# First chunk of gated linear attention into four experts: loading keys and values as fp32 by GpSimd's queue, with the whole order of the work searched anew

## The chip, the cores and the metric

The kernel runs on one core of one Trainium2 chip. The metric is the time of one execution on the device in microseconds (us), the median of several executions. The engines are named as in the profile: PE is TensorE's matmul and PEld its weight load, DVE is VectorE, ACT is ScalarE, POOL is GpSimd and SP is SyncE, which here only issues DMAs. DMAs issued by SP go into the queue that the profile calls hardware_dynamic, those issued by POOL into the one that it calls software_dynamic.

## What is computed

A recurrent attention with a forget gate, and behind it a mixture of four experts with dense routing. The inputs and the output are fp32, and the kernel feeds its matmuls in bf16.

```python
# q, k, v, f_logit: (4 batches, 8 heads, 768 steps, 48)
f = 1 / (1 + exp(-f_logit))
for t in range(768):
    state = f[:, :, t, :, None] * state + k[t] (outer) v[t]     # 48 x 48 per batch and head
    y[:, :, t] = q[t] @ state
x = y with the heads side by side                              # 3072 x 384
p = probs / (probs.sum(-1) + 1e-9)
out = sum over 4 experts of p[:, e] * (relu(x @ w1[e]) @ w2[e])   # w1 384 x 1024, w2 1024 x 384
```

## The kernel before

**Tiling.** The 768 steps are cut into six chunks of 128. Within a chunk the recurrence is turned into matmuls, batch by batch (b = 0 to 3): running sums of log f (`pe_cs` with the triangular matrix Up or Ub, and for the first chunk also `pe_cq`), their exponentials on ACT (`exps`, `expq`), scaled copies of q and k (`product`, on DVE or POOL), their transposes on PE (`pe_tp`) and a copy out of PSUM into QK, the 128 x 128 score blocks (`pe_at`) which are evicted with a causal mask (`ev_at`, or a plain copy and then `mask_at` on POOL), and the scores times v (`pe_y`). The state between chunks is kept in Sf and its bf16 copy Sb (`pe_kv`, `ev_kv`, `state`). The outputs y are transposed again (`pe_xt`, `dma_xt` or `dma_xs`) and go into the experts: `mm_h`, `relu`, `mm_o` for the first two chunks, and for later ones forms that save multiplications with sums of blocks (`mm_p1`, `mm_hs`, `mm_l1`, `mm_p`).

**The first chunk (c = 0)** is special, since nothing can hide it. Its loads are cut by batch. f and q come in pairs of neighbouring steps (`PAIRED`), in pieces of 384 bytes. k comes by SP in pieces of 192 bytes. v comes by POOL, which casts it to bf16 in the DMA and writes the tile vb that the matmuls read. POOL's v issues 0 and 1 wait for the landings of k1 and k2 (`GATE`).

**What sets the order.** All work is recorded as a list of about 1,550 operations in a planner (`Plan`), each with a cost per engine, dependencies, and the buffers that it takes and frees. A table of numbers, `RANKS`, gives each operation its place (a letter behind a number also fixes its engine). The planner walks the list in that order, chooses buffers, and then emits the instructions in that order, so that every engine's instruction stream is the table's order. An engine runs its stream strictly in sequence: an instruction that waits holds up all behind it. `ORDER` is the order of the first chunk's loads on SP, `SEQ` that of POOL's DMA issues (v0 to v3 and the first weights w0, w1; w2 to w10 follow).

**Weights.** w0 to w3 are halves of w1 of experts 0 and 1, w4 and w5 are the halves of w2 of expert 0, w6 to w10 are whole matrices. All are cast to bf16 in POOL's DMAs, as they always were. The gate's load of the second chunk (f, batches 1 of the first half) waits for w8.

**Fillers.** `FILLER` places extra matmuls of a constant tile into a spare PSUM bank ahead of named operations on PE: six ahead of cs 0.0 (the first running sum) and four ahead of tpk 0.1. Nothing reads what they write.

Of the kernel before, what the change touches and what calls it, by code (L numbers as in the profile page):

```python
# [11 lines left out]
ALU = mybir.AluOpType  # L12
# [64 lines left out]
)  # L77
FILLER = {"cs 0.0": 6, "tpk 0.1": 4}


class Op:
# [10 lines left out]
class Plan:  # L92
# [20 lines left out]
    def run(self):  # L113
# [7 lines left out]
        for o in done:  # L121
            (e, cost), = o.costs.items()
            t = free_at[e]
# [1081 lines left out]
```

## Time and profile before

| what | value |
|---|---|
| time, median of 3 runs | 286.37 us (286.18 to 286.67) |
| the profiled execution's own time | 285.82 us |
| its span, from the first instruction to the last event | 284.1 us |
| PE busy | 276.0 us, 97% of the span |
| DVE, POOL, ACT busy | 208.7, 185.3, 178.2 us |
| DMA packets | 153688, 41.88 MB |

How to read it: the profile has one row for a stretch of equal instructions, with the start, the length, the engine, the line of the kernel, what is written and from what, and in brackets the engine's idle time just before and what ended it. A matmul's recorded length includes its way through the array, so that matmuls in sequence overlap; the distance between the starts of two rows is what the stretch cost. Idle time of an engine that nobody waits for costs nothing.

### The profile page before, as it was taken

What the parts mean: (1) busy time and instruction counts of PE and PEld (TensorE: products, weight loads), DVE (VectorE), ACT (ScalarE), POOL (GpSimd) and SP (SyncE); (2) the same over time, 40 slices, a digit from 0 to 9 for tenths busy, and PEclk for the clock granted to TensorE, in tenths of its full rate; (3) what the DMA queues carried; (4) which work ended last, traced back from release to release, by engine and by line L of the source; (5) the groups of instructions that cost most, each with busy time, mean ns of one, the idle gap of its engine ahead of it and who ended that gap; (6) DMA issues with size and microseconds to landing.
All of it is one profiled execution on the core that took longest, in us unless ns stands there. A gap on an engine that the chain in (4) does not pass through costs nothing.

```text
span 284.1 us, 8015 instructions
## 1 busy us (share of the span) xinstructions
PE 276.0 (97%) x3228; PEld 241.2 (85%) x3228; DVE 208.7 (73%) x437; ACT 178.2 (63%) x350; POOL 185.3 (65%) x197
## 2 busy tenths in 40 slices
PE   6889999999999999999999999999999999999995
PEld 4678565668788999999998999999999899999995
DVE  5695487797779587769887786686765687857683
ACT  5668235647898848686866867769367456556420
POOL 5799353706699878667729955695656545793761
PEclk9999999999999999999999999999999999999999
DMA  6999999999988999999999999996547015201003
GB/s 156 189 195 205 208 195 200 184 216 181 162 150 159 198 164 208 204 168 184 194 175 207 194 179 218 184 166 124 111 82 160 30 31 76 67 0 59 2 2 111
DMA packets 153688, 41.88 MB, mean 147 GB/s; under 512 B 144028, under 2 KB 152860, under 8 KB 153652
## 3 DMA queue, kind: packets, MB, share of 16 engines
q1 hardware_dynamic: 142404, 34.66, 65.1%
q0 software_dynamic: 11248, 6.72, 16.8%
q8 instruction: 25, 0.41, 0.6%
q14 instruction: 11, 0.09, 0.1%
HBM read 31.51 MB, written 4.72 MB: 128 GB/s over the span
## 4 chain that ended last, share of the span: by engine, by line
PE 84%; DMA 9%; POOL 4%; ACT 1%; DVE 1%; issue 0%; ACTq 0%; POOLq 0%
PE ps_m L646 29%; PE ps_m L531 26%; PE ps_m L574 7%; DMA w_sb<-in_moe_w_dram 7%; PE ps_m L514 6%; PE ps_m L499 4%; PE ps_m L654 2%; DMA f<-in_f_logit_dram 2%; PE ps_m L437 2%; POOL w_sb L312 2%; PE ps_m L464 1%; PE ps_m L460 1%; PE ps_m L347 1%; PE ps_m L470 1%; POOL AT L441 1%; PE ps_m L362 1%
## 5 line engine op out<-in xcount | busy, mean ns | idle before, releaser
L531 PE MATMUL ps_m<-x,w_sb 128*128 128x256 bf16 x672 | 84.3, 273 | 0.0
L531 PEld LDWEIGHTS <-w_sb 128*128 128x128 bf16 x672 | 63.6, 98 | 7.1
L595 ACT ACTIVATE h<-ps_m 128x512 bf16<-128x512 f32 x82 | 46.8, 600 | 24.1 <-PE ps_m L531 23.9
L646 PEld LDWEIGHTS <-S 128*128 128x128 bf16 x576 | 48.2, 98 | 0.8
L673 DVE TENSOR_TENSOR o<-ps_m,o 128x192 f32<-128x192 f32 x91 | 31.1, 353 | 19.1 <-PE ps_m L646 17.3
L646 PEld LDWEIGHTS <-h 128*128 128x128 bf16 x432 | 36.2, 98 | 0.8
L610 POOL TENSOR_TENSOR S<-h 128x1024 bf16<-128x1024 bf16 x14 | 29.7, 2124 | 10.3 <-DVE S L610 6.3
L499 PE MATMUL ps_m<-x,w_sb 128*128 128x128 bf16 (+2 forms) x264 | 35.1, 282 | 0.0
L420 ACT ACTIVATE yb<-ps_m,pn 128x384 bf16<-128x384 f32 x55 | 29.4, 586 | 8.5 <-PE ps_m L464 5.6
L397 POOL TENSOR_TENSOR qk<-q,e 128x384 bf16<-128x384 f32 x18 | 21.6, 1201 | 12.5 <-DVE f L549 3.9
L646 PE MATMUL ps_m<-ts_sb,S 128*128 128x192 bf16 x288 | 29.3, 246 | 0.0
L646 PE MATMUL ps_m<-w_sb,h 128*128 128x192 bf16 x288 | 29.2, 246 | 0.0
L646 PE MATMUL ps_m<-w_sb,S 128*128 128x192 bf16 x288 | 28.7, 246 | 0.0
L499 PEld LDWEIGHTS <-w_sb 128*128 128x128 bf16 x264 | 21.6, 98 | 8.1
L593 DVE TENSOR_SCALAR h<-ps_m 128x512 bf16<-128x512 f32 x30 | 20.6, 688 | 9.6 <-PE ps_m L531 8.5
L453 DVE TENSOR_TENSOR AT<-ps_m,mask 128x512 bf16<-128x512 f32 x40 | 25.6, 682 | 2.1 <-PE ps_m L437 2.0
L510 ACT ACTIVATE h<-ps_m 128x512 bf16<-128x512 f32 x33 | 19.1, 595 | 12.2 <-PE ps_m L499 11.8
L380 ACT ACTIVATE e<-ps_m 128x384 f32<-128x384 f32 x40 | 23.6, 708 | 3.2 <-PE ps_m L347 1.4
L610 POOL TENSOR_TENSOR S<-h,S 128x1024 bf16<-128x1024 bf16 x10 | 21.2, 2124 | 4.5 <-DVE o L673 2.5
L514 PE MATMUL ps_m<-w_sb,h 128*128 128x384 bf16 x128 | 23.9, 326 | 0.0
L585 DVE CUSTOM_DVE_ANT_0 h<-ps_m,QK 128x512 bf16<-128x512 f32 x24 | 16.0, 686 | 5.1 <-PE ps_m L574 1.9
L588 ACT COPY QK<-ps_m 128x512 f32<-128x512 f32 x24 | 13.8, 588 | 8.1 <-PE ps_m L574 5.2
(140 smaller groups left out, 523.3 us busy)
## 6 DMA issues: line engine op xcount, KB each, us to landing
out_dram<-o SPq DMA_DIRECT2D x23, 192.0 KB, 2.5
w_sb<-in_moe_w_dram POOLq DMA_DIRECT2D x5, 768.0 KB, 15.2
k<-in_k_dram SPq DMA_DIRECT2D x10, 384.0 KB, 5.1
q<-in_q_dram SPq DMA_DIRECT2D x10, 384.0 KB, 5.0
v<-in_v_dram SPq DMA_DIRECT2D x10, 384.0 KB, 5.1
f<-in_f_logit_dram SPq DMA_DIRECT2D x9, 384.0 KB, 5.8
w_sb<-in_moe_w_dram POOLq DMA_DIRECT2D x6, 384.0 KB, 8.2
f<-in_f_logit_dram SPq DMA_DIRECT2D x6, 192.0 KB, 4.4
```

Of the source, the lines that this page charges most:

```text
L380: nc.scalar.activation(out=o, in_=i, func=AF.Exp, scale=1.0 if j else -1.0)
L397: return engines[eng].tensor_tensor(out=tl("qk", c, b)[:, j, :, 0:D].rearrange("t (i r) d -> t i r d", r=2), in0=tl("qk"[j], c, b // 2)[:, ...
L420: nc.scalar.activation(out=ys, in_=y, func=AF.Copy, scale=pe)
L453: nc.vector.tensor_tensor(out=tl("AT", c, b)[:, r].rearrange("s i t -> s (i t)"), in0=tl("A", c, b, r).rearrange("s i t -> s (i t)"), in1= ...
L499: nc.tensor.matmul(out=hp(c, e, fc, n0, n1, nf)[:, f], lhsT=w1_sb[:, e, kk, (fc + f) * 128:(fc + f + 1) * 128], rhs=tl("xT", c)[:, kk, n0: ...
L514: nc.tensor.matmul(out=tl("op", c, e, nt)[:, 0:Din], lhsT=tl("h", c, e, half_of(c, nt * T))[:, fc, nt * T:(nt + 1) * T], rhs=w2_sb[:, e, f ...
L531: nc.tensor.matmul(out=out_[:, f], lhsT=w1_sb[:, e, kk, (fc + f) * 128:(fc + f + 1) * 128], rhs=tl("xs", c, hf, p)[:, el, kk, :], start=(k ...
L593: nc.vector.tensor_relu(out=dst, in_=tl("hp", c, hf, p, el, fc))
L595: nc.scalar.activation(out=dst, in_=tl("hp", c, hf, p, el, fc), func=AF.Relu)
L610: return engines[eng].tensor_tensor(out=o, in0=in0, in1=in1, op=op)
L646: nc.tensor.matmul(out=out_, lhsT=lhs[:, f, :], rhs=rhs[:, f, :], start=(first and el == 0 and f == 0), stop=(el == 1 and f == KH - 1), sk ...
L673: nc.vector.tensor_tensor(out=o, in0=src, in1=o, op=ALU.add)
```

## The change

In words:

- In the first chunk, k and v are both loaded as fp32 by POOL's DMAs, 8 loads of 192 KB, into the tiles k and v. v is cast to bf16 on chip by `cast_v` (one batch on ACT, one on DVE, two on POOL). SP is left with f and q, in the order f0 q0 f1 q1 f2 f3 q2 q3.
- POOL's issues begin directly behind the four selects for Up. The mask's select and the select for Ub stand between the second and the third issue; the constant fills ahead of them (Ub, the three e tiles, the mask) move from POOL to DVE. The evictions that use the mask, and the sums that use Ub, depend on these selects.
- The waits of `GATE` are gone.
- `RANKS` is a new table, so that the order on all engines is another one in the whole program.
- The fillers are 13: six ahead of cq 0.0, three ahead of cs 0.3, two ahead of tpq 0.2 and two ahead of y 0.1.

```diff
 RANKS = (
-    "0 9 14 1 5 18 3 27 2 21 33 48 19 40 24 52 30 61 36 71 42 84 55 95 63 109 74 121 80 137 88 151 97 163 169 106 165 114 184 "
+    "0 1 2 13 19 38 52 71 3 10 4 18 5 6 7 20 9 44 12 61 14 66 15 75 64 83 74 84 77 85 78 86 79 125 103 126 106 127 107 141 "
...
-FILLER = {"cs 0.0": 6, "tpk 0.1": 4}
+FILLER = {"cq 0.0": 6, "cs 0.3": 3, "tpq 0.2": 2, "y 0.1": 2}
...
     Ub = const.tile([T, T], BF16)
-    nc.gpsimd.memset(Ub, 1.0)
-    nc.gpsimd.affine_select(out=Ub, in_=Ub, compare_op=ALU.is_ge, fill=0.0, base=0, channel_multiplier=-1, pattern=[[1, T]])
+    nc.vector.memset(Ub, 1.0)
+    def make_ub():
+        return nc.gpsimd.affine_select(out=Ub, in_=Ub, compare_op=ALU.is_ge, fill=0.0, base=0, channel_multiplier=-1, pattern=[[1, T]])
...
-        nc.gpsimd.memset(pads["e", i][:, 0:2 * NP * P2].rearrange("t (r d i) -> t r d i", r=2, i=NP)[:, :, D:P2, :], 0.0)
+        nc.vector.memset(pads["e", i][:, 0:2 * NP * P2].rearrange("t (r d i) -> t r d i", r=2, i=NP)[:, :, D:P2, :], 0.0)
...
-    nc.gpsimd.memset(mask01, 1.0)
-    nc.gpsimd.affine_select(
+    nc.vector.memset(mask01, 1.0)
+    def make_mask():
+        return nc.gpsimd.affine_select(
...
     def load(c, nm, b, n):
-        if (c, nm) == (0, "v"):
-            ins[c, nm, b] = nc.gpsimd.dma_start(out=tl("vb", c, b), in_=srcs[nm][c, :, b * H:(b + n) * H, :])
-            if f"v{b}" in GATE:
-                after(ins[c, nm, b], ins[GATE[f"v{b}"]])
+        if c == 0 and nm in "kv":
+            ins[c, nm, b] = nc.gpsimd.dma_start(out=tl(nm, c, b // 2)[:, hh(b, n), :], in_=srcs[nm][c, :, b * H:(b + n) * H, :])
             return
...
+        if j == 2:
+            masked = P.add("mask", {"POOL": 0.9}, lambda e: make_mask(), -599, deps=issued[-1:])
+            upper = P.add("ub", {"POOL": 0.3}, lambda e: make_ub(), -100, deps=[masked])
+            issued.append(upper)
...
-            vb = ld[0, "v", b] if c == 0 else P.add(f"v {c}.{b}", {"POOL": 0.52, "ACT": 0.54}, one(cast_v), s(4),
+            vb = P.add(f"v {c}.{b}", {"POOL": 0.52, "ACT": 0.54} if c else {"POOL": 0.52, "ACT": 0.54, "DVE": 0.34}, one(cast_v), s(4),
                        deps=[ld[c, "v", b]], takes=[("vb", c, b)], frees=[("v", c, half)])
...
-ORDER = "f0 k0 q0 f1 k1 q1 f2 f3 k2 q2 k3 q3"
-SEQ = "v0 v1 v2 w0 v3 w1"
+ORDER = "f0 q0 f1 q1 f2 f3 q2 q3"
+SEQ = "k0 k1 k2 v0 k3 v1 w0 v2 w1 v3"
-GATE = {"v0": (0, "k", 1), "v1": (0, "k", 2)}
```

What the change moves is seen in the instruction streams. POOL's stream behind the selects for Up, before (Ub and the mask, then the loads of v, which write vb):

```order
L202 AFFINE_SELECT Up_79<-par_77 128x128 x4
L205 MEMSET Ub_85 128x128
L206 AFFINE_SELECT Ub_85<-Ub_85 128x128
L217 MEMSET e0_102 128x2x64
L219 MEMSET mask01_108 128x512
L220 AFFINE_SELECT mask01_108<-mask01_108 128x512
L293 DMA vb0_181<-in_v_dram 128x8x48
L312 DMA w1_sb_119<-in_moe_w1_dram 128x3x512
L293 DMA vb3_237<-in_v_dram 128x8x48
```

The same place now (k0 and k1 are tiles of two batches each, so that the first row is two loads; v0 and v1 likewise):

```order
L202 AFFINE_SELECT Up_79<-par_77 128x128 x4
L301 DMA k0_126<-in_k_dram 128x8x48 x2
L227 AFFINE_SELECT mask01_107<-mask01_107 128x512
L209 AFFINE_SELECT Ub_85<-Ub_85 128x128
L301 DMA k1_131<-in_k_dram 128x8x48
L301 DMA v0_134<-in_v_dram 128x8x48
L318 DMA w1_sb_117<-in_moe_w1_dram 128x3x512
L296 CAST vb0_261<-v0_134 128x384
L301 DMA v1_290<-in_v_dram 128x8x48
L445 AFFINE_SELECT AT1_282<-AT1_282 128x512
```

The loads of k now stand directly behind Up, and the first cast of v stands ahead of the third load of v and the second weight. On PE, before, between the running sums of batch 1 and the first scores (the last row; each kind of row is shown once, where it begins; S5 is the fillers' tile, gp the log gates, qk the scaled q and k, QK their transposes):

```order
L351 MATMUL ps_m2_160<-gp0_88,Up_79 128x192
L362 MATMUL ps_m3_172<-gp0_88,Wp_80 128x192
L1156 MATMUL ps_m7_122<-S5_69 128x512
L406 MATMUL ps_m4_197<-ident_72,qk0_92 128x128
L362 MATMUL ps_m5_202<-gp1_90,Wp_80 128x192
L406 MATMUL ps_m6_209<-ident_72,qk1_94 128x128
L351 MATMUL ps_m0_216<-gp1_90,Up_79 128x192
L437 MATMUL ps_m2_245<-QK0_235 128x128
```

And now, from the same sums to the first y (AT are the masked scores):

```order
L355 MATMUL ps_m2_171<-gp0_87,Up_79 128x192
L366 MATMUL ps_m3_183<-gp0_87,Wp_80 128x192
L410 MATMUL ps_m4_188<-ident_72,qk0_91 128x128
L410 MATMUL ps_m5_200<-ident_72,qk1_93 128x128
L441 MATMUL ps_m6_215<-QK0_212 128x128
L366 MATMUL ps_m0_228<-gp1_89,Wp_80 128x192
L355 MATMUL ps_m2_237<-gp1_89,Up_79 128x192
L441 MATMUL ps_m3_251<-QK1_226 128x128
L1161 MATMUL ps_m7_120<-S5_69 128x512
L355 MATMUL ps_m5_266<-gp1_89,Up_79 128x192
L468 MATMUL ps_m6_295<-vb0_261,AT0_233 128x48
```

The four fillers between the sums of batch 1 and the first transposes are gone; the sums of batch 2 (gp1 with Wp and Up) now stand behind the first scores, and three fillers stand ahead of the sums of batch 3.

More of the change, by code (lines that the diff above doesn't have):

```diff
@@ L117, in run @@
                 self.left[k] = self.left.get(k, 0) + 1
-        free_at = {"DMA": 0.8, "DVE": 5.0, "POOL": 3.5, "ACT": 2.1, "PE": 2.0}
+        free_at = {"DMA": 0.8, "DVE": 6.0, "POOL": 2.9, "ACT": 2.1, "PE": 2.0}
         rooms = {r: [(0.0, s) for s in slots] for r, slots in self.rooms.items()}
@@ L216 @@
         pads["e", i] = const.tile([T, 2 * NP * P2 + HD], FP32, name=f"e{i}")
-        nc.gpsimd.memset(pads["e", i][:, 0:2 * NP * P2].rearrange("t (r d i) -> t r d i", r=2, i=NP)[:, :, D:P2, :], 0.0)
+        nc.vector.memset(pads["e", i][:, 0:2 * NP * P2].rearrange("t (r d i) -> t r d i", r=2, i=NP)[:, :, D:P2, :], 0.0)
     mask01 = const.tile([T, NP * T], BF16)
-    nc.gpsimd.memset(mask01, 1.0)
-    nc.gpsimd.affine_select(
-        out=mask01, in_=mask01, compare_op=ALU.is_ge, fill=0.0,
-        base=0, channel_multiplier=-1, pattern=[[0, NP], [1, T]],
-    )
+    nc.vector.memset(mask01, 1.0)
+    def make_mask():
+        return nc.gpsimd.affine_select(
+            out=mask01, in_=mask01, compare_op=ALU.is_ge, fill=0.0,
+            base=0, channel_multiplier=-1, pattern=[[0, NP], [1, T]],
+        )
     Sf = const.tile([MP, B, NP, D], FP32)
@@ L312, in load_w @@
         ins["w", i] = nc.gpsimd.dma_start(out=w[:, e, ks, cols], in_=r[e][:, ks, cols])
-        if f"w{i}" in GATE:
-            after(ins["w", i], ins[GATE[f"w{i}"]])
         if i == w_last:
@@ L689 @@
     issued, late = [], {(0, x[0], int(x[1])): i for i in LATE for x in LATE[i].split()}
-    def gate(x):
-        return [ld[GATE[x]]] if x in GATE else []
     for i, x in enumerate(ORDER.split()):
-        add_load(0, x[0], int(x[1]), 1, -1000 + i)
+        add_load(0, x[0], int(x[1]), 1, -1000 + i, deps=[o for o in P.ops[-1:] if i])
     every = slice(0, None)
@@ L704 @@
         i = int(x[1:])
-        if x[0] == "v":
-            issued.append(P.add(f"v issue {i}", {"POOL": 0.8}, lambda _, i=i: load(0, "v", i, 1), -600 + 2 * j,
-                                deps=issued[-1:] + gate(x), takes=[("vb", 0, i)], lag=1.2))
-            ld[0, "v", i] = P.add(f"ld v0.{i}", {"DMA": 1.45}, lambda _: None, VW[0] + j, deps=issued[-1:] + fifo[-1:], lag=2.0)
-            fifo.append(ld[0, "v", i])
+        if j == 2:
+            masked = P.add("mask", {"POOL": 0.9}, lambda e: make_mask(), -599, deps=issued[-1:])
+            upper = P.add("ub", {"POOL": 0.3}, lambda e: make_ub(), -100, deps=[masked])
+            issued.append(upper)
+        if x[0] != "w":
+            issued.append(P.add(f"{x[0]} issue {i}", {"POOL": 0.95}, lambda _, i=i, nm=x[0]: load(0, nm, i, 1), -600 + 2 * j,
+                                deps=issued[-1:], takes=[(x[0], 0, i // 2)], lag=1.2))
+            ld[0, x[0], i] = P.add(f"ld {x[0]}0.{i}", {"DMA": 0.6}, lambda _: None, VW[0] + j, deps=issued[-1:] + fifo[-1:], lag=2.0)
+            fifo.append(ld[0, x[0], i])
             continue
@@ L717 @@
         iss = P.add(f"w issue {i}", {"POOL": 0.8}, lambda _, i=i, x=(e, which, ks, cols): load_w(i, *x),
-                    -600 + 2 * j, deps=issued[-1:] + gate(x) + ([ld[1, "k", 0]] if i == w_last else []), lag=1.5)
+                    -600 + 2 * j, deps=issued[-1:] + ([ld[1, "k", 0]] if i == w_last else []), lag=1.5)
         op = P.add(f"w {i}", {"DMA": 1.95 if i < 6 else 4.05}, lambda _: None, -400 if i == w_last else (VW[1] if i < 2 else -480) + j, deps=[iss] + fifo[-1:], lag=1.0)
@@ L754, in attention @@
             cs = P.add(f"cs {c}.{b}", {"PE": 0.165 if c else 0.45}, on(pe_cs), s(0),
-                       deps=[G[b]], takes=[pt_("cs")], lag=0.2, frees=[("gp", c, half)])
+                       deps=[G[b]] + ([upper] if c else []), takes=[pt_("cs")], lag=0.2, frees=[("gp", c, half)])
             ex = P.add(f"exps {c}.{b}", {"ACT": 1.19 if c else 0.56}, on(exps), s(0) + 0.1, deps=[cs],
@@ L794, in attention @@
             at, vb = AT_[b], VB[b]
-            eA = [P.add(f"ev_at{r} {c}.{b}", {"ACT": 0.735} if c == 0 and f"{b}.{r}" in BYPOOL.split() else {"DVE": 0.685 if c else 0.73}, one(ev_at, r), s(7) + 0.1 + 0.1 * r, deps=[at],
+            eA = [P.add(f"ev_at{r} {c}.{b}", {"ACT": 0.735} if c == 0 and f"{b}.{r}" in BYPOOL.split() else {"DVE": 0.685 if c else 0.73}, one(ev_at, r), s(7) + 0.1 + 0.1 * r, deps=[at, masked],
                         takes=[("AT", c, b)], frees=[pt_("A", r)]) for r in range(2)]
```

120 rows, old and new, of the table RANKS are left out of this document.

## The prediction, made before the result was known

> **What bounds the kernel now.** I read PE's busy time by stage first, since the page gives it 97% of the span. The columns are the stage's borders, its length, PE's busy time and instructions, the clock column, and the DMAs' share and rate.
>
> ```profile
> core 0: us, PE busy (x), PEclk, DMA share, GB/s
> 4.96:11.72 6.76, 6.76 (x56) 1.00 1.09 216
> 11.72:18.89 7.17, 5.09 (x86) 1.00 1.69 179
> 18.89:26.05 7.16, 7.16 (x141) 1.00 1.27 206
> 26.05:47.95 21.90, 21.90 (x139) 1.00 1.18 199
> 47.95:60.00 12.05, 11.37 (x107) 1.00 1.17 201
> 60.00:270.00 210.00, 210.00 (x2572) 1.00 0.77 140
> ```
>
> From 18.89, where the first expert matmul starts, PE is busy without idle time to the end, but for 0.68 us behind 47.95. The matmuls behind that point are the same before and after. So the change can move the end in two ways only: by the moment at which PE's dense work begins, and by the 0.68 us. I take 26.05, where expert 1's first matmul starts, as the mark: all attention work of chunk 0 lies before it.
>
> The start is seen in PE's and DVE's timelines (start, length, engine and line, what is written, count, idle time before and its end).
>
> ```profile
> 7.68 1.92 PE L1156 MATMUL ps_m<-S 128*128 128x512 bf16 x4
> 9.39 0.63 PE L406 MATMUL ps_m<-ident,qk 128*128 128x128 bf16 x4
> 9.82 0.85 PE L362 MATMUL ps_m<-gp,Wp 128*128 128x192 bf16 x4
> 10.46 0.55 PE L406 MATMUL ps_m<-ident,qk 128*128 128x128 bf16 x4
> 10.85 0.49 PE L351 MATMUL ps_m<-gp,Up 128*128 128x192 bf16 x4
> 11.18 0.24 PE L355 MATMUL ps_m<-par,gp 128*128 128x2 bf16 x4
> 12.45 0.41 PE L437 MATMUL ps_m<-QK 48*128 48x128 bf16 x8 [0.56 <-DVE QK L288]
> ```
>
> ```profile
> 7.79 1.10 DVE L397 TENSOR_TENSOR qk<-k,e 128x384 bf16<-128x384 f32 x2 [2.83 <-ACT e L382]
> 9.36 1.26 DVE L394 TENSOR_TENSOR qk<-q,e 128x384 bf16<-128x384 f32 x2 [0.47 <-ACT e L387]
> 11.70 0.69 DVE L288 COPY QK<-ps_m 112x1024 bf16<-112x1024 bf16 x1 [1.08 <-PE ps_m L406]
> ```
>
> The first scores start at 12.45. They wait for DVE's copy at 11.70, that one for PE's transposes, which wait for the products of k and q, and the first product waits not for k but for ACT (its bracket). So k is in time now. The rows also show PE's clock doubling: four matmuls of 192 columns take 0.64 us at 9.82 (start to next start) and 0.33 us at 10.85, although the clock column prints 1.00.
>
> The 0.68 us lie at the end of a chain of waits (start, length, what):
>
> ```profile
> 22.65 18.79 DMA w_sb<-in_moe_w_dram
> ...
> 41.45 5.70 DMA f<-in_f_logit_dram
> ...
> 48.11 0.85 ACT gp L342
> ...
> 49.01 0.48 PE ps_m L347 x2
> ```
>
> w8 lands at 41.44, the second chunk's f may load only then, and PE stands at 49.01 for the gate. This chain is bound by the stream of DMAs, not by PE.
>
> **The change, part by part.** *Constants.* Five fills go from POOL to DVE. They fall into the 2.83 us that DVE sits idle before 7.79 and cost nothing; if the products of k ever started as soon as the fills end, they would stand in front. *k by POOL.* The rows that set it, of POOL's timeline and of the DMA view:
>
> ```profile
> 1.76 1.04 POOL L202 TENSOR_SCALAR_AFFINE_SELECT Up<-par 128x128 bf16<-128x128 bf16 x4 [0.39 <-DVE par L197]
> ...
> 7.87 2.85 POOL L293 DMA_DIRECT2D vb<-in_v_dram  x3 [2.94 <-DMA k<-in_k_dram]
> ```
>
> ```profile
> k<-in_k_dram SPq DMA_DIRECT2D x3, 192.0 KB, 3.7
> ```
>
> ```profile
> DMA packets 1865, 0.67 MB, mean 232 GB/s; under 512 B 1865, under 2 KB 1865, under 8 KB 1865
> ...
> q0 software_dynamic: 77, 0.01, 4.8%
> ...
> vb<-in_v_dram POOLq DMA_DIRECT2D x3, 96.0 KB, 6.9
> ```
>
> The first row of DMAs is from the view of 0.5 to 7.8 us, the others from that of 7.8 to 10.7: sizes, and the median time from issue to landing. POOL can issue k0 at 2.80, where Up ends, and k1 0.95 later (v's three issues take 2.85 together). As SP's loads go, k0 would land at 2.80 + 3.7 = 6.5; as POOL's do now, at 2.80 + 6.9 = 9.7. SP's queue is as full of f and q then as it is in the second view, and by 10.7 POOL's queue has moved 77 packets, 2.8 us after v0's issue began: about 2.4 us go by before the first bytes. From 5.2 on k0's 196.6 kB then share 232 GB/s with SP: at half of it 1.7 us, that is 6.9, and some time for the end of the load. I take 8.3, between that and POOL's own row, and 9.9 for k1, one such load later (bounds 7.5 and 10.7).
>
> DVE's stream is now k0, q0, k1, q1, copy, copy. From k1 at 9.9: 0.55 for k1, 0.6 for q1, 0.69 for the first copy of QK, so the first scores start at 11.8 instead of 12.45. That is 0.65 us earlier; by k1's bounds and the same steps the scores start between 9.4 and 12.6.
>
> *PE from there to the mark.* Before: 26.05 - 12.45 = 13.6 us, of which 2.08 are idle between 11.72 and 18.89 (7.17 - 5.09) and 0.56 of these ahead of the scores. With the part of each wait that the recorded end of a matmul hides I put the waits behind 12.45 at 2.0 and the work at 11.6. After: the same 11.6, plus the sums of batch 2, which now stand behind the scores (at full clock 0.33 for Up, 0.1 for par behind it, and 0.32, half of 0.64, for Wp), plus seven fillers: 0.43 each at the slow clock (7.68 to 9.39 for four), half that at the full one, 1.5. Sum 13.85; if PE never waits and runs at full clock the mark is at 25.65, **0.4 us earlier**.
>
> *The clock.* This is the term that I think decides. Windows of 3.4 us around the doubling (same columns as above):
>
> ```profile
> 3.96:7.37 3.41, 2.71 (x24) 1.00 1.12 236
> 7.37:10.78 3.41, 3.41 (x20) 1.00 0.99 229
> ```
>
> PE was busy 79% of the first (2.71 of 3.41) and stayed slow. It was busy without a gap from 4.96, and the clock doubled at 10.8, 5.8 us later. What closed the gap was the four fillers from 7.68 to 9.39. They are gone. After the change the sums of batches 0 and 1 end near 8.1, the transposes of batch 0 wait for k0 until about 9, those of batch 1 for k1 until about 10.6, and the scores start at 11.8: four groups of 0.43 us in 3.7 us, half busy. The gapless stretch begins at 11.8, so by the row the clock doubles at 17.6, and 5.8 us of work run at half speed: 2.9 us lost. Some of that falls where PE would wait at full clock (2.0 us of waits before; the three groups of fillers already sit in such places). I take 1.2 off and charge **+1.7 us** (bounds 0, if the clock is full in time, and 2.9). The Trainium skill, "TensorE: Matmul & The Clock Gate", section "Part 1: The HAM clock gate", says that the clock is released after one busy window of about 3.4 us, that the window runs freely, and that the loss should stay under 1% of a span. The two rows agree with it as far as they go; by its 3.4 us alone, counted from 11.8, the loss would be 1.7 us instead of 2.9, 0.5 with the same 1.2 off, and the sum below would give 285.8.
>
> *v as fp32 and cast on chip.* The view of 10.5 to 13.0 us, when v's cast loads run beside SP's:
>
> ```profile
> DMA packets 2251, 0.35 MB, mean 141 GB/s; under 512 B 2251, under 2 KB 2251, under 8 KB 2251
> ...
> q0 software_dynamic: 1216, 0.12, 89.9%
> q1 hardware_dynamic: 1035, 0.24, 63.7%
> ```
>
> At 232 GB/s SP's 0.24 MB would take 1.0 us; the other 1.5 us moved 1216 of v's packets, 1024 to a load: 1.2 us each, against 0.85 for 196.6 kB at 232 GB/s. Four loads save up to 1.4 us of the stream. New gaps take some back, since the cast of v0 waits on POOL for its landing with v2's and w1's issues behind it, and the mask of batch 1 with w2's. I take 1.0 (bounds 0 and 1.4): the gate is ready near 48.0. POOL's two casts take 0.5 us each and are otherwise beside other work:
>
> ```profile
> L288 POOL CAST vb<-v x10: 493/498/1138, 54.4 to 196.5; 128x384 bf16<-128x384 f32 x10
> ```
>
> *Sum.* The mark comes 1.7 - 0.4 = 1.3 us later. PE then reaches 47.95 at 49.25, when the gate is ready even if the stream gains nothing, so the 0.68 us wait goes: +0.6 us in all. The profiled execution took 285.82 us (span 284.1 and 1.7 around it): 286.4 by that one; it lies 0.55 under the median of 286.37, so **287.0 us**. The rest of the new order I cost at nothing: PE's list has the same 35 blocks from the mark to the second chunk's sums, and PE's full occupancy covers it as long as the buffers hold.
>
> **Rivals.**
> *The clock is full by 12 us* (faster). Its place is PE between 4.96 and 11.8. If the sums and the transposes count as busy enough, or if k lands as SP's loads do and closes the gaps, nothing of the 1.7 is charged. The mark is 0.4 earlier, and the gate at 48.0 now decides: the sums of chunk 1 start there instead of at 49.01, 1.0 us earlier: 285.3. It decides as soon as less than about 0.7 us of half-speed work is left behind the scores. For it: the sums keep PE busy for 3.1 us from 4.96; against it: 79% was not enough in the window that ended at 7.37.
> *The stream gains nothing* (no change). Then the gate still comes at 48.96, and any gain at the mark is waited away at the same place: 286.4, if the mark moves less than 0.7 us later. For it: under the cast the DMAs are busy throughout, and new waits sit ahead of the weights on POOL.
> *k0 and k1 land together, near 10.7* (slower). Then q0, k1, q1 and the copy follow each other on DVE, the scores start at 13.0, and everything above comes 1.2 later: 288.2. For it: v0 and v1 are issued back to back and the median landing is 6.9 us.
>
> **How the numbers follow.** The forecast gets 0.42, the full clock 0.30, the stream without gain 0.15, k late 0.13. Within the forecast, a share of about 0.13 ends within 0.2% (0.57 us, about what a measurement of this kernel can tell from no change). Faster: 0.30 of the rival, and 0.02. Within 0.2%: 0.13 and 0.12. Slower: the rest of the forecast, 0.27, the late k's 0.13, and 0.03 where the stream gains nothing and the mark is late. The range reaches down to 285.0 (full clock, and the stream's bound of 1.4 at the gate, which caps any gain from an earlier k) and up to 288.5 (late k, 288.2; the forecast with nothing taken off the 2.9 us is 288.2 too).
>
> **What would show it.** In the changed profile: matmuls of 192 columns behind the first scores taking 0.16 us from start to start (right) or 0.08 (wrong); the first scores near 11.8; expert 1's first matmul near 27.4; no idle time ahead of the sums of chunk 1 near 49; w8 landing near 40.4. A new idle stretch on PE behind 60 us would make the prediction wrong in a place that I costed at nothing.

## The result, and the profile after

The changed kernel took 287.94 us (median of four executions, 287.89 to 288.25) against 286.49 (286.18 to 286.67) for the kernel before, run beside it: a ratio of 1.0054, 95% interval 1.0037 to 1.0072. It is slower, by about 1.45 us. The profiled execution took 287.96 us, with a span of 285.9.

PE's stages of the changed kernel, in the columns that the prediction used. The borders are 4.96 as before, the first scores, the first expert matmul, the mark, the end of the matmuls ahead of the sums of chunk 1, and the last of these sums.

```profile
core 0: us, PE busy (x), PEclk, DMA share, GB/s
4.96:11.81 6.85, 5.22 (x41) 1.00 1.14 262
11.81:19.52 7.71, 7.71 (x102) 1.00 1.05 192
19.52:26.98 7.46, 7.37 (x142) 1.00 1.18 188
26.98:49.09 22.11, 22.11 (x143) 1.00 1.18 199
49.09:62.05 12.96, 12.10 (x113) 1.00 1.12 188
62.05:270.00 207.95, 207.95 (x2542) 1.00 0.74 141
```

The first scores start 0.64 us earlier than before (12.45 became 11.81), the first expert matmul 0.63 later (18.89, 19.52), and the mark 0.92 later (26.06, 26.98). Behind the mark the change moved two things. PE's timeline there:

```profile
49.57 0.32 PE L351 MATMUL ps_m<-gp,Ub 128*128 128x384 bf16 x1 [0.32 <-ACT gp L346]
50.05 0.32 PE L351 MATMUL ps_m<-gp,Ub 128*128 128x384 bf16 x1 [0.16 <-ACT h L514]
...
61.18 0.21 PE L468 MATMUL ps_m<-vb,AT 128*128 128x48 bf16 x2 [0.38 <-ACT vb L295]
```

The brackets count from the recorded end of the matmul before. Counted from start to start, less the time of its columns, the three waits are 0.48, 0.32 and 0.54 us, and 0.16 behind the last (between 61.49 and 61.67). Before, there was one wait of 0.85 in all this. So 0.92 at the mark and 1.50 - 0.85 = 0.65 behind it give 1.57; PE's last matmul starts 1.55 later (280.75, 282.30), and the stores behind it end 0.27 later still: the span's 1.8 us. The profiled executions themselves are 2.1 us apart (285.82, 287.96): 0.3 us of the difference lies outside the span.

The chain of waits shows where the last two come from:

```profile
25.15 16.82 DMA w_sb<-in_moe_w_dram
41.98 0.02 issue
41.99 5.72 DMA f<-in_f_logit_dram
...
48.65 0.32 SPq L307
...
49.15 11.44 DMA v<-in_v_dram
60.59 0.02 issue
60.61 0.52 ACT vb L295
```

w8 lands at 41.98, 0.54 later than before, not earlier. Chunk 1's first v, which landed at 52.19 before, is now issued behind the f of the second half, at 49.15, and lands at 60.59.

### The profile page after: what moved, and what is told of

Same layout as the page of the kernel before. It is cut to its first block, busy times and chain, and to the rows that moved or that the text cites. A ratio compares the mean times of both kernels' runs of the same rounds, so it can differ in the third digit from the quotient of the medians.

```text
span 285.9 us, 8025 instructions
## 1 busy us (share of the span) xinstructions
PE 277.7 (97%) x3231; PEld 241.9 (85%) x3231; DVE 212.6 (74%) x452; ACT 175.1 (61%) x343; POOL 187.7 (66%) x197
## 4 chain that ended last, share of the span: by engine, by line
PE 81%; DMA 14%; POOL 2%; DVE 1%; ACT 0%; issue 0%; SPq 0%; DVEq 0%; ACTq 0%
PE ps_m L650 29%; PE ps_m L535 26%; PE ps_m L578 7%; DMA w_sb<-in_moe_w_dram 6%; DMA v<-in_v_dram 4%; PE ps_m L503 4%; PE ps_m L518 4%; PE ps_m L441 2%; DMA k<-in_k_dram 2%; DMA f<-in_f_logit_dram 2%; PE ps_m L658 2%; PE ps_m L468 2%; PE ps_m L464 1%; PE ps_m L474 1%; PE ps_m L351 1%; POOL w_sb L318 1%
## 5 line engine op out<-in xcount | busy, mean ns | idle before, releaser
L599 ACT ACTIVATE h<-ps_m 128x512 bf16<-128x512 f32 x77 | 44.2, 596 | 27.0 <-PE ps_m L535 25.3
L614 POOL TENSOR_TENSOR S<-h 128x1024 bf16<-128x1024 bf16 x11 | 23.4, 2124 | 10.2 <-ACT h L599 3.2
L597 DVE TENSOR_SCALAR h<-ps_m 128x512 bf16<-128x512 f32 x35 | 23.9, 685 | 7.7 <-PE ps_m L535 7.6
L424 ACT ACTIVATE yb<-ps_m,pn 128x384 bf16<-128x384 f32 x53 | 28.4, 584 | 1.1 <-PE ps_m L468 0.8
L401 POOL TENSOR_TENSOR qk<-q,e 128x384 bf16<-128x384 f32 x17 | 20.3, 1195 | 10.4 <-DVE qk L401 4.0
L514 ACT ACTIVATE h<-ps_m 128x512 bf16<-128x512 f32 x31 | 17.7, 598 | 10.5 <-PE ps_m L503 9.2
L490 POOL TENSOR_TENSOR Sf<-Sf,egs 112x192 f32<-112x192 f32 (+1 forms) x21 | 12.7, 605 | 16.9 <-DVE S L614 9.0
L614 POOL TENSOR_TENSOR S<-S,h 128x1024 bf16<-128x1024 bf16 x8 | 17.0, 2124 | 6.5 <-DVE S L614 3.0
```

The source lines that it names most:

```text
L401: return engines[eng].tensor_tensor(out=tl("qk", c, b)[:, j, :, 0:D].rearrange("t (i r) d -> t i r d", r=2), in0=tl("qk"[j], c, b // 2)[:, ...
L424: nc.scalar.activation(out=ys, in_=y, func=AF.Copy, scale=pe)
L597: nc.vector.tensor_relu(out=dst, in_=tl("hp", c, hf, p, el, fc))
L599: nc.scalar.activation(out=dst, in_=tl("hp", c, hf, p, el, fc), func=AF.Relu)
L614: return engines[eng].tensor_tensor(out=o, in0=in0, in1=in1, op=op)
```

## The experiments

In the profiles of these runs PE's clock first doubles between 4.3 and 17.6 us, each time at another moment. So one profile shows one draw of the clock, single executions of a kernel spread over 1.5 us or more, and the times below are medians, with the ratio to the kernel before on the same chip and its interval. (The ratio on record is not the plain quotient of the two medians; the two differ by up to 0.15%.)

**Four more fillers at the start (a_clk).**

```diff
-FILLER = {"cq 0.0": 6, "cs 0.3": 3, "tpq 0.2": 2, "y 0.1": 2}
+FILLER = {"cq 0.0": 6, "tpk 0.0": 2, "tpk 0.1": 2, "cs 0.3": 3, "tpq 0.2": 2, "y 0.1": 2}
```

> The changed kernel with four more fillers on PE, two ahead of the first transposes of k and two ahead of the second, so that PE has no gap from 6.9 us to the first scores. Account A (the end is set at three places: the mark at 26.98, the wait for the gate at 49, the wait for v at 60.6; the last two end when a DMA lands): the clock doubles near 10.8 instead of 14.2, the 2.4 us of half-speed work behind the first scores take 1.2 less, of which waits eat about half, and the mark comes near 26.4. The gate is still ready near 49.5 and v still lands near 60.6, so that the time stays within 0.2 us of 287.9 and the wait ahead of the chunk-1 sums grows from 0.8 to about 1.4. Rival B (PE's dense work alone sets the end): the time falls by what the mark gains, about 0.6, to 287.3. Rival C (the clock was not what made the mark late): the mark stays at 27.0.

Times: 288.31 us against 286.16, 1.0060 (1.0034 to 1.0085). In the profile the clock doubles at 8.55 and the mark comes at 25.29, 1.7 before that of the changed kernel. (This execution took 286.37 us, the shortest of the twelve; in the median nothing is gained.) But w8 comes at 40.43 and the gate at 48.1, 1.5 earlier as well, and PE waits there for 1.05 us. Account A said that DMAs hold these two; they moved with the mark instead. The reason is POOL's stream (of the changed kernel, with the weights' issues at L318):

```profile
9.21 0.75 POOL L318 DMA_DIRECT2D w_sb<-in_moe_w_dram  x1
13.54 0.50 POOL L296 CAST vb<-v 128x384 bf16<-128x384 f32 x1 [3.57 <-DMA v<-in_v_dram]
14.01 0.93 POOL L301 DMA_DIRECT2D v<-in_v_dram  x1
14.94 0.75 POOL L318 DMA_DIRECT2D w_sb<-in_moe_w_dram  x1
...
20.05 1.02 POOL L445 TENSOR_SCALAR_AFFINE_SELECT AT<-AT 128x512 bf16<-128x512 bf16 x1 [1.35 <-ACT AT L449]
21.02 0.79 POOL L318 DMA_DIRECT2D w_sb<-in_moe_w_dram  x1
```

w4 is issued at 21.02, behind a mask that waits for batch 2's scores. When attention is late, the weights are.

**v of chunk 1 ahead of f again (a_vload).** The table gives an operation's place by name.

```diff
+MOVE = {"ld v1.0": 243.5}
...
-        op.prio = int(rank.rstrip("ADP"))
+        op.prio = MOVE.get(op.name, int(rank.rstrip("ADP")))
```

> The changed kernel with one load moved in SP's stream: v of chunk 1's first half stands ahead of f of its second half again, as it did before the change. Account A: v lands near 52 instead of 60.6, the wait of 0.53 us ahead of the first product with v goes, with the 0.13 behind it, and the time falls by 0.5 to 0.66, to 287.3 to 287.4; f of the second half lands near 59 as before the change and nobody waits for it. Rival D (the load is only the last of several late things): another wait takes its place within 5 us and the time stays within 0.2 of 287.9.

Times: 290.54 us against 286.16, 1.0144 (1.0095 to 1.0194): slower by a further 0.5 to 0.9% (1.0054 and 1.0097 are the changed kernel's own ratios), which neither account had. The chain and PE's timeline of this kernel:

```profile
49.20 11.79 DMA f<-in_f_logit_dram
61.02 0.85 ACT f L338
61.89 0.85 ACT gp L346
...
62.79 0.32 PE ps_m L351
```

v lands at 52.98, but now f is the load that takes 11.8 us, and the sums at L351, which the new order has at 60.4, wait 2.1 us for the gate made from it. Whichever load is issued near 49, beside the last weights, lands near 60 (before the change it was f too, at 59.18, and its sums stood at 62.78). The stages around it:

```profile
core 0: us, PE busy (x), PEclk, DMA share, GB/s
56.90:60.31 3.41, 3.41 (x33) 1.00 1.17 203
60.31:63.72 3.41, 1.42 (x18) 1.00 0.89 179
63.72:67.13 3.41, 3.41 (x24) 0.50 1.29 222
67.13:70.50 3.37, 3.37 (x33) 1.00 0.44 73
```

Behind the wait the clock column falls to 0.50 for 3.41 us: the wait costs another 1.7.

**The gate's load behind w7 (a_gate7), and all three edits (a_three).**

```diff
-    w_last, w_gate = len(pieces) - 1, len(pieces) - 3
+    w_last, w_gate = len(pieces) - 1, len(pieces) - 4
```

> The changed kernel with the second load of f of chunk 1 waiting for weight w7 instead of w8, so that it is issued 4.3 us earlier (37.7 instead of 42.0). Account A: the gate is ready near 45, before PE asks for it at 49.1, so that the wait of 0.8 us there goes; the loads behind it on SP, v among them, come some 4 us earlier as well, so that the wait of 0.66 at 60.6 goes too: 286.4 to 286.6 in all. If v still comes late, only the 0.8: 287.1. Rival E (w8 and w9 land some 3 us later in exchange, and experts 2 and 3 wait for them): 287.9 or more, with a new wait for weights between 45 and 60.

> The changed kernel with all three edits: four more fillers, v's load ahead of f's, and the gate's load behind w7. Account A: with both waits for DMAs gone the mark decides, so that the fillers' gain of about 0.6, worth nothing alone, now shows: 287.9 - 0.8 - 0.66 - 0.6 = 285.8, below the kernel before (286.4). Rival B (each edit is worth the same whatever the others do): the sum of the three single gains. Rival C (the clock is not the cause): the same as the better of the two load edits together, about 286.4.

Times: 288.26 (1.0078, 1.0051 to 1.0106) and 290.75 us (1.0149, 1.0113 to 1.0185) against 286.16. Issued at 39.16, f takes 10.05 us instead of 5.72 and lands at 49.21: beside two weights instead of one it lands later than the changed kernel's 47.71, though issued 2.8 earlier, and v lands at 61.82. The wait ahead of the sums is 1.72 us. In a_three a wait of 2.07 us stands at 60.6, as in a_vload. Account A fell in all three parts. What stays is that the loads behind 38 us share the DMAs with w8, w9 and w10, and that moving these loads among themselves gained nothing; what an earlier stream of weights does is seen below (a_front).

**The changed kernel again, and three single edits, on a second chip.** Base:

> The changed kernel itself once more, as the base for the others on this chip, and to see how its time spreads. In six profiles so far PE's clock doubles at 4.5, 8.6, 10.8, 14.2, 15.6 and 15.9 us, that is on a grid of 3.413 us whose phase differs from execution to execution. Account A2 (the phase decides how much of the start runs at half speed, and the weights' issues on POOL, which wait for attention work, move with it, so that the gate and v move too): the median is 287.9 as before, ratio 1.005 or so, single executions spread over 1.5 us or more; if the profile has the doubling later than 14.2 the mark is later than 26.98 by about half the difference, and w8, the gate and the last matmul move by about the same. Rival (DMA landings are fixed): w8 lands near 42.0 whatever the mark does.

Times: 288.92 us against 286.36, 1.0097 (1.0069 to 1.0125). In the profile the clock doubles at 17.11, the mark is at 28.12, w8 at 43.13 and the last matmul at 283.42: the stream moves with the mark, as account A2 said.

*w4 and w5 ahead of the mask* (a_issue):

```diff
+MOVE = {"w issue 4": 99.5, "w issue 5": 99.6}
```

> The changed kernel with the issues of weights w4 and w5 moved ahead of batch 2's mask on POOL, where they wait for nothing that attention computes: w4 is issued at 18.7 instead of 21.0, w5 at 19.4 instead of 22.3, as close to their places before the change (18.1, 18.9). Account A2: the gap in the stream between w3 and w4 closes, w4 lands near 27.6 instead of 28.6, w8 1.0 earlier near 41.0, the gate is ready at 48.5 when PE comes at 49.1, v lands near 59.6, so that both waits (0.8 and 0.66) go for the larger part: 286.7, -1.2 against the changed kernel. Rival B: the mask of batch 2, 1.5 us later than before in POOL's stream, holds up the scores of batch 2 and the mark by as much: no gain or a loss. Rival D: the stream is full anyway, w8 stays near 42: no change.

Times: 288.05 us, 1.0070 (1.0050 to 1.0090). w4 is issued at 18.80, and from w1 to w4 the stream takes 6.9 us instead of 7.9. But w1 itself lands 0.6 later, w8 stays at 41.97, and the waits stay (0.66 and 0.73). So this gap was real and not the only one.

*Without the seven later fillers* (a_nofill):

```diff
-FILLER = {"cq 0.0": 6, "cs 0.3": 3, "tpq 0.2": 2, "y 0.1": 2}
+FILLER = {"cq 0.0": 6}
```

> The changed kernel with only the six fillers at its start; the seven behind the scores, which I charged with 1.5 us of PE, are gone. If they stand in places where PE would wait anyway (account A2, from the waits of 0.12 to 0.15 us ahead of them and the ACT work behind), the mark stays within 0.2 of the changed kernel's at the same clock phase and the time within 0.3. If they are work in PE's path (the prediction's sum), the mark comes up to 1.5 earlier and the time falls by as much, to about 286.5. If they hold the clock (rival C), the doubling comes one step of 3.4 us later in some executions, or a second half-speed stretch appears, and the time rises by 0.5 to 1.5.

Times: 287.25 us, 1.0030 (1.0006 to 1.0053), against 1.0097 for a_same on the same chip, with intervals that don't meet. PE's timeline from the scores of batch 1 to the sums of batch 3, of a_same:

```profile
13.55 0.61 PE L441 MATMUL ps_m<-QK 48*128 48x128 bf16 x8
14.49 1.06 PE L1161 MATMUL ps_m<-S 128*128 128x512 bf16 x2 [0.33 <-issue]
15.35 0.85 PE L355 MATMUL ps_m<-gp,Up 128*128 128x192 bf16 x4
```

and of a_nofill:

```profile
14.10 0.61 PE L441 MATMUL ps_m<-QK 48*128 48x128 bf16 x8
14.64 0.82 PE L355 MATMUL ps_m<-gp,Up 128*128 128x192 bf16 x4
```

From scores to sums it takes 1.80 us with three fillers (one of them has no record) and 0.54 without: 1.26 us for the three at half speed, and there is no wait in their place. The mark is at 27.07 with the clock doubling at 17.58, against 28.12 at 17.11.

*The kernel before without its four fillers* (b_clk):

```diff
-FILLER = {"cs 0.0": 6, "tpk 0.1": 4}
+FILLER = {"cs 0.0": 6}
```

> The kernel before without the four fillers ahead of its first transposes, all else as it was: the part of the change that the prediction took for the decisive one, alone. With them PE has no gap from 4.96 to 11.7, so that a whole step of the grid is busy and the clock has doubled by 11.8 at the latest. Without them there is a gap of about 1.5 us near 8.5, and the doubling comes in 11.8 to 15.2 unless the sums suffice. Account A2: half of up to 3.4 us more at half speed, partly in waits: +0.5 to +1.0 us, 286.7 to 287.2, and the weights move with it. If the clock costs nothing (rival C): within 0.2 of 286.2.

Times: 286.23 us against 286.36, 1.0003 (0.9981 to 1.0025). The clock is late (17.30), and its matmuls run at half speed:

```profile
13.94 0.82 PE L351 MATMUL ps_m<-gp,Up 128*128 128x192 bf16 x4
14.55 0.29 PE L355 MATMUL ps_m<-par,gp 128*128 128x2 bf16 x4
14.71 0.80 PE L362 MATMUL ps_m<-gp,Wp 128*128 128x192 bf16 x4
```

Four matmuls of 192 columns take 0.61 us from start to start here, and 0.33 in the prediction's rows. Yet the mark is at 26.09, as in the profile of before with the clock at 10.79 (26.06). In the old order the waits take it all up. This one execution was the shortest of the twelve, but the median says the same: rival C is right.

**Issues forward on POOL (a_front), and with four early fillers (a_best), on a third chip.** Both leave out the seven fillers.

```diff
+FILLER = {"cq 0.0": 6}
+MOVE = {"v issue 2": 53.5, "w issue 1": 53.6, "w issue 4": 99.5, "w issue 5": 99.6}
```

a_best has `{"cq 0.0": 6, "tpk 0.0": 2, "tpk 0.1": 2}` for its fillers.

> The changed kernel without the seven later fillers (base: 1.0030 of the kernel before) and with four issues moved forward on POOL: v2 and w1 ahead of the cast of v0, into the 3.6 us in which POOL waits for v0 to land, and w4 and w5 ahead of batch 2's mask. Account A3 (the weights' stream runs dry twice, once behind w0 because v2 and w1 are issued only behind the cast, near 14, and once behind w3): w1 lands near 19.3 instead of 20.7, w8 near 41.0 instead of 42.2, the gate's wait of 0.9 at 49 goes, v lands near 59.5 and its wait shrinks: ratio 1.000, within 0.3 us of the kernel before. Rival B (POOL's larger share starves SP's queue): q3 lands 1 us or more later than 17.6, and the mark comes as much later than 27.1: no gain. Rival D: w8 stays at 42 again, since bytes and not issues set it: 1.003.

> The same as the one without the seven fillers and with the four issues forward, and with two fillers ahead of the first and two ahead of the second transposes, so that PE has no gap up to the first scores and a whole step of the clock's grid is busy by 11.8 at the latest. Account A3: the clock doubles between 8 and 12 in any phase, the mark comes near 25.6, and since the weights no longer wait for attention work, both gains hold: 0.995 to 0.998 of the kernel before. Rival (the clock costs nothing where waits stand anyway, as in the kernel before without its fillers): the same as without these fillers, near 1.000.

Times: 285.95 us (1.0006, 0.9977 to 1.0035) and 286.01 us (1.0000, 0.9971 to 1.0029) against 285.62. POOL's stream in a_front:

```profile
9.20 0.75 POOL L318 DMA_DIRECT2D w_sb<-in_moe_w_dram  x1
9.93 0.93 POOL L301 DMA_DIRECT2D v<-in_v_dram  x1
10.86 0.76 POOL L318 DMA_DIRECT2D w_sb<-in_moe_w_dram  x1
13.49 0.50 POOL L296 CAST vb<-v 128x384 bf16<-128x384 f32 x1 [1.87 <-DVE AT L453]
```

What the DMAs moved behind w0 in the changed kernel (start and end, length, POOL's busy time and instructions, clock, DMA share, GB/s):

```profile
16.00:18.00 2.00, 2.00 (x4) 1.00 0.88 147
...
24.00:26.00 2.00, 1.98 (x4) 1.00 1.19 167
```

and in a_front:

```profile
16.00:18.00 2.00, 2.00 (x4) 0.50 1.15 210
...
24.00:26.00 2.00, 0.00 (x0) 1.00 1.31 202
```

Both dips are filled (in a_nofill, the base of this edit, the rates are 173 and 145). w8 lands at 40.98, v of chunk 1 at 59.28, and PE has no idle time from 47 to 62, in a_front first and in the changed kernel below:

```profile
47.00:62.00 15.00, 15.00 (x140) 1.00 1.11 190
```

```profile
47.00:62.00 15.00, 14.14 (x130) 1.00 1.07 185
```

This profile of a_front fell into a bad draw of the clock: it fell back to half speed from 11.76 to 22.00, with the mark at 28.52. So PE comes late to the places of both waits, and this profile alone can't tell what the earlier landings did to them; a_best's can. Rival B is seen too: q3 lands at 18.75, later than in any other run. In a_best's profile (clock doubling at 8.63) the mark is early, at 25.67, w8 lands at 39.94, PE passes to the sums of chunk 1 at 47.78 without a wait, and 0.16 us near 59 are all that is left of the waits behind the mark. In a_clk, with a mark as early (25.29) and the issues where they were, they were 1.57 us. a_best's median is no better than a_front's, so that the early fillers are worth nothing that these runs can tell.

**v cast in the DMA again (a_vcast), k on SP again (a_ksp), both without the seven fillers.**

```diff
+    v16 = lambda b: tl("v", 0, b // 2)[:, hh(b), :].bitcast(BF16)[:, :, 0:D]
...
-            ins[c, nm, b] = nc.gpsimd.dma_start(out=tl(nm, c, b // 2)[:, hh(b, n), :], ...
+            ins[c, nm, b] = nc.gpsimd.dma_start(out=v16(b) if nm == "v" else tl(nm, c, b // 2)[:, hh(b, n), :], ...
...
-        return copy(eng, tl("vb", c, b), tl("v", c, b // 2)[:, hh(b), :])
+        return copy(eng, tl("vb", c, b), tl("v", c, b // 2)[:, hh(b), :] if c else v16(b))
```

```diff
+MOVE = {"k issue 0": 0.5, "k issue 1": 2.5, "k issue 2": 38.5, "v issue 0": 38.55, ...
...
-            ins[c, nm, b] = nc.gpsimd.dma_start(...
+            ins[c, nm, b] = (nc.sync if nm == "k" else nc.gpsimd).dma_start(...
+            if nm == "v" and b < 2:
+                after(ins[c, nm, b], ins[0, "k", b + 1])
```

> The changed kernel without the seven later fillers, with v of the first chunk cast to bf16 in the DMA again (into the same place, and then copied on chip by the engines that cast it, so that order and waits stay). Account A3 (v as fp32 gives the stream about 1.1 us at w0, and the order of issues loses it again): w0 lands near 18.4 instead of 17.4, q2 and q3 earlier than 15.3 and 17.6 since POOL's packets are small again, w8 near 43, and the time rises by about 0.5 to 1.0 us over the base, ratio 1.005 to 1.006. Rival (v as fp32 in packets of 4 KB takes SP's share, so that q3 and the mark come late): q3 near 16, the mark 0.5 to 1 earlier, the time no higher than the base, 1.000 to 1.003.

> The changed kernel without the seven later fillers, with k on SP's queue again (f0 k0 q0 f1 k1 q1 f2 f3 k2 k3 q2 q3) and v0 and v1 waiting for k1 and k2 as before the change. Account A3 (k by POOL brings the first scores 0.64 forward, and the mark keeps little of it): first scores near 12.4 instead of 11.8, the v's 2 us later, the cast of v0 and the issues behind it on POOL too, so that w8 comes near 43 and the time rises by 0.5 to 1.0: 1.005 to 1.006. Rival (loading k by POOL is worth nothing, since batches 2 and 3, whose q come late, set the mark): q2 and q3 no earlier, time within 0.3 us of the base.

a_vcast: 287.99 us against 285.62, 1.0068 (1.0042 to 1.0094). That is the range of account A3, but the interval overlaps that of a_nofill (1.0006 to 1.0053, on another chip), so that a rise isn't shown, and the steps are not account A3's: w0 lands at 16.13, earlier than a_nofill's 17.37, and w8 at 42.21 as in a_nofill (42.20). q3 does come early, at 13.02, but the mark, at 26.90, hardly: in this profile PE waits 0.85 us near 20.5, until w1 lands at 21.30. The profiled execution took 287.53 us, less than that of a_nofill (288.19), so that it does not show where a higher median would come from; this stays open.

a_ksp: 286.46 us, 1.0024 (1.0000 to 1.0048), as a_nofill's 1.0030. k1 lands at 7.37 on SP's queue, 2.7 us earlier than POOL's in the changed kernel, DVE waits for no k ahead of the scores, and the first scores start at 11.02, not at 12.4. So the new order starts the first scores earlier without POOL's queue for k, and loading k by POOL is worth nothing that these intervals can tell. (It is one profile, with full speed from 4.35 to 7.76, which shortened the sums of batch 0; a_best, with k by POOL and full speed from 8.63, starts the scores at 10.81. The edit also issues w0 3.1 us later, at 12.32; it lands at 17.40, as in a_nofill.)

## Why the prediction was right, and which steps were not

The numbers that the points rest on, one profile each (PE's clock, the last time that it rises; the mark; w8's landing; PE's waits near 49 and 60 from start to start), with the ratio of the times:

| kernel | full speed from | mark | w8 | waits | ratio |
|---|---|---|---|---|---|
| before | 10.79 | 26.06 | 41.44 | 0.85, 0 | 1 |
| b_clk | 17.30 | 26.09 | 40.79 | 0, 0 | 1.0003 |
| changed | 14.18 | 26.98 | 41.98 | 0.80, 0.70 | 1.0054 |
| a_same | 17.11 | 28.12 | 43.13 | 0.79, 0.69 | 1.0097 |
| a_clk | 8.55 | 25.29 | 40.43 | 1.05, 0.52 | 1.0060 |
| a_nofill | 17.58 | 27.07 | 42.20 | 0.90, 0.50 | 1.0030 |
| a_front | 22.00 | 28.52 | 40.98 | 0, 0 | 1.0006 |
| a_best | 8.63 | 25.67 | 39.94 | 0, 0.16 | 1.0000 |

*What bounds it: right, but one place short.* PE's end did move by the mark and the waits behind it alone. The prediction named two places; the third, at 60.6, it had put among the things costed at nothing ("a new idle stretch on PE behind 60 us" was its sign of error, and it came: 0.70 us).

*k by POOL and the first scores: right in number.* k0 at 8.28 (said 8.3), k1 at 10.03 (9.9), scores at 11.81 (11.8). The wait ahead of the second product of k in the changed kernel's DVE stream is for k1, as said:

```profile
10.12 0.56 DVE L401 TENSOR_TENSOR qk<-k,e 128x384 bf16<-128x384 f32 x1 [0.72 <-DMA k<-in_k_dram]
```

So the path is right: k1's landing sets the scores. But k's new queue is not what made them earlier than before: a_ksp, with k on SP, starts them no later.

*The mark: right in sign, 0.92 against 1.3, from wrongly split terms.* The prediction charged 1.5 us for the fillers at full clock and 1.7 for the clock, as if the second were a price of missing fillers. b_clk shows that the missing fillers alone cost nothing in the old order. In the changed kernel's own profile the seven new fillers ran at full speed and took 0.66, 0.43 and 0.44 us, 1.5 in all, as charged; and both speeds that the prediction named as signs are there: four matmuls of 192 columns take 0.61 us at 12.35 and 0.33 at 14.96. Half speed lasted 2.4 us behind the first scores (11.81 to 14.18) and so cost 1.2 us at most, not 1.7. Where the clock is later the fillers cost more: they stand in PE's path, and at half speed they take 0.42 us each instead of 0.21. With them the mark follows the clock (from 14.18 to 17.11 it goes from 26.98 to 28.12, 0.4 us for each us); without them, 17.58 gives 27.07. The rule "5.8 us of gapless work until the clock doubles" fell: it doubled at 14.18, 2.4 us after the scores. The bound from the Trainium skill that the prediction had set beside it, "TensorE: Matmul & The Clock Gate", "Part 1: The HAM clock gate", a window of about 3.4 us that runs freely, is the one that these traces bear out.

*The stream: wrong, and the step that failed.* The prediction said that v as fp32 brings the stream 1.0 us forward, that "new gaps take some back", and that the gate is ready at 48.0, w8 at 40.4, so that the 0.68 us wait goes. At w0 a gain is there (17.47 instead of 18.67), but not by the step that was named: w0 is issued 1.5 us earlier (9.21, 10.69) and takes no less from issue to landing (8.26 us, 7.98), and in a_vcast, with v cast in the DMA again, it takes 6.93. So no run shows that v as fp32 frees the stream. Then v2 and w1 are issued behind the cast at 14.0 and w4 behind the mask at 21.0, the DMAs run at 147 and 167 GB/s there, and w4 lands 1.25 us later than before (28.59, 27.34). From w0, 1.20 early, to w8, 0.54 late, the stream lost 1.7 us, where up to 0.4 was left for gaps. a_front and a_best show it: with the four issues forward w8 comes at 40.98 and 39.94, and in a_best the waits behind an early mark are 0.16 us.

*The sum.* In the span it came out as 0.92 + 0.65 + 0.27 (the stores, uncosted) where 1.3 - 0.68 had been said. The direction holds. That the median (287.94 against 287.0) lies in the range is in part luck, since errors offset each other: the mark moved 0.4 us less than said, the waits behind it 1.3 us more. In the ratios, leaving out the seven fillers takes 1.0097 to 1.0030, and the issues forward to 1.0006; the second step is shown by the traces, its worth in time lies within the intervals. The two together are clear of them: 0.9977 to 1.0035 for a_front, 1.0037 to 1.0072 and 1.0069 to 1.0125 for the changed kernel. No version beat the kernel before by more than can be told.

*Outside the span: a term that was taken as fixed.* The prediction put "1.7 around" the span also after the change. Every execution on record of the changed kernel and of its variants took 1.96 to 2.12 us more than its span, and every one of the kernel before and of b_clk 1.66 to 1.78. So 0.3 of the 1.45 us lie where the profile doesn't reach, and no run here tells their cause. They are also what is left of the loss in a_front: the median of its spans is 283.9 us, as for the kernel before on that chip, and its times are 285.95 against 285.62.

## What to carry to other kernels

Ask of every filler whether PE would wait in its place also when the clock is slow: there, inputs that would be late are ready, and the filler is pure work at twice its price. A DMA that an engine issues is as late as whatever that engine waits for ahead of it; put issues in front of casts and masks that wait, and follow a stream to its last consumer before you credit it with a gain at its start. Compare the time less the span of two kernels, too: what differs there stands in no row of the profile. Where a load must land beside weights, moving another load into its place only changes which one is late.

## What the hardware showed

*The clock moves on a grid of 3.413 us whose phase differs from execution to execution.* In each trace the changes of the clock lie whole multiples of 3.413 us apart (one step in a_vload's rows above, 80 steps at full speed in the changed kernel). I counted, for each step of the grid in fourteen profiles, the columns of the matmuls that start in it, each weighted by the part of the 128 x 128 array that it uses, over what the step could stream at its speed. Of 48 steps at half speed, all eleven with a share of 0.78 or more were followed by full speed, none below 0.74 was, and between 0.74 and 0.77 both happened (7 and 8 times). At full speed, the four steps with 0.21 to 0.29 were followed by half speed, and none with 0.38 or more. The weights matter: by columns alone, six steps with a share of 0.84 or more stayed at half speed, so that scores with 48 rows count for less than the columns that they stream. And a wait of about 2 us can cost a further 1.7: in a_vload it left its step a share of 0.24, in a_three, where it reached over a border of the grid, 0.42, and the clock held.

*Loads without a cast move in large packets on POOL's queue, and SP's loads lose by it.* The DMA views from 8.5 to 17 us, of the changed kernel and of a_vcast:

```profile
DMA packets 1945, 1.88 MB, mean 222 GB/s; under 512 B 1284, under 2 KB 1682, under 8 KB 1944
```

```profile
DMA packets 4945, 1.62 MB, mean 191 GB/s; under 512 B 4429, under 2 KB 4824, under 8 KB 4944
```

The eight loads of k and v are 384 packets of 3840 or 4224 bytes, at about 255 ns; with the cast, v moves in 4096 packets of 96 bytes at 30 ns. q3 on SP's queue, issued near 6.6, lands between 15.0 and 18.8 in the ten profiles with fp32 loads of k and v by POOL, and at 13.02 in a_vcast. The Trainium skill's page "DMA: Bandwidth & Descriptors", section "Queues, rings and completion order", says that an engine takes turns between queues packet by packet; by that the queue with the larger packets gets the larger share, and the landings of q3 agree.
